# One copy for turned keys and queries, stores by head half, and gathers ahead of the sums in a fused attention and expert kernel

## The chip, the cores and the metric

The kernel runs on one core of a Trainium2 chip, in one launch. The metric is the device time of the execution in microseconds, as a median of several runs. TensorE (PE) multiplies matrices and turns tiles, VectorE (DVE) and ScalarE (ACT) work on tiles lane by lane, GpSimd (POOL) does the same for tiles in SBUF, and SyncE (SP) issues transfers. Each engine takes its instructions in program order and waits for the others by semaphores.

## What is computed

Random feature attention over 8 batches of 8 heads with 576 rows of 64 columns each, whose output goes as 4608 rows of 512 columns into a layer of 8 experts with one expert for each row:

```python
def phi(x):
    proj = np.einsum('bhsd,md->bhsm', x, omega)
    return np.concatenate([np.cos(proj), np.sin(proj)], axis=-1) / np.sqrt(m)
q_p, k_p = (phi(q), phi(k))
kv = np.einsum('bhsm,bhsd->bhmd', k_p, v)
z = np.sum(k_p, axis=2)
num = np.einsum('bhsm,bhmd->bhsd', q_p, kv)
den = np.einsum('bhsm,bhm->bhs', q_p, z)      # |den| kept from zero
x = (num / den)                               # to rows of 512
# experts, on rows x of 512:
logits = xn @ en.T / tau                      # xn, en: rows over their norms
expert_idx = np.argmax(logits, axis=1)
gate_w = probs[np.arange(N), expert_idx]      # softmax of the logits
out[mask] = gate_w[mask, None] * (np.maximum(x[mask] @ w1[e], 0.0) @ w2[e])
```

## The kernel before, in words

**The attention loop.** 32 steps, one for two heads of one batch (head i on partitions 0 to 63, head i + 4 on 64 to 127), run as a pipeline in a loop over n from 0 to 32 (line 1050). The instructions of each engine stand in the order in which the code is written. In iteration n a step's keys and values are multiplied (kv_products(n)), the step before it gets its numerators (num(n - 1), norm(n - 1)), and the step behind it has its keys projected and waved (proj_k(n + 1), frac, wave). "Step n" below is iteration n; VectorE's copy of kvT (line 301) is close to its start.

The raw keys and queries of a step lie in one tile kq; TensorE turns them into PSUM (turns, line 177), from where the projections need them in SBUF. VectorE copies the first 512 columns (copy_k, tile kT, line 189) and ScalarE the other 640 (copy_q, tile qT, line 195). They are read by proj_q and proj_k of the next iteration (lines 208, 225, 234). After the turn ScalarE also makes the sine of the keys (wave, snk) ahead of its copy and their cosine (cok) behind it; VectorE makes the whole turns' remainder (frac, line 251), its absolute value (fold, line 257), and the norm (lines 373 to 375).

The sums of the features over the sequence (z) are made by GpSimd: zsum (lines 277 to 281) adds the nine blocks of snk, then those of cok, in ten instructions; z_turn(n) of the next iteration takes them to TensorE. GpSimd also copies the finished rows to fp16 (to_rows, line 390), sums the logits (sums, lines 422, 424), and issues one of 32 weight pieces in each iteration (weights_in, lines 92 and 98). The order at the end of an iteration is to_rows(n - 1), sums(n - 1), weights_in(n), zsum(n + 1), gathers.

**Routing beside it.** When half of the batches are through, the rows of these are given to experts, in pieces of a few VectorE instructions each, that lie in iterations 9 to 31 (lay_first, line 986; the dictionary pieces). The first piece of an iteration runs ahead of z_turn and kv_out (piece_now), the others behind them (all_pieces). The first 11 of 43 blocks of 128 rows are known then.

**Hand-over.** The rows of the attention go through DRAM: store_rows (line 426) sends a pair of steps from tile xb to x_rows by SP, in odd iterations, two transfers (one for each half of the heads) in a row. gather(j) (line 830) fetches the 128 rows of block j into one of three buffers xin_all by an indirect DMA that GpSimd issues. The same buffers hold v of odd steps until step 29. turn_x(j) (line 867) turns a block on TensorE and copies it to xT by VectorE. In iteration 32 the first block's matmuls begin (hidden(0)).

**Experts.** 43 blocks: hidden(j), 32 matmuls (line 913), result(j), 8 matmuls (line 934), with gathers three blocks ahead, and results scattered to the output by GpSimd (line 947).

The gathers of the first five blocks stand here:

```python
            if NS - 2 <= n < NS:
                turn_x(n + 2 - NS, "dve")
...
            weights_in(n)
            if nx:
                zsum(n + 1, 0)
                zsum(n + 1, 1)
            if n == NS - 3:
                gather(0)
            elif n == NS - 2:
                gather(1)
                gather(2)
```

Of the kernel before, what the change touches and what calls it, by code (L numbers as in the profile page):

```python
# [11 lines left out]
FP32 = mybir.dt.float32  # L12
# [3 lines left out]
I16 = mybir.dt.int16  # L16
AF = mybir.ActivationFunctionType
# [11 lines left out]
def kernel(  # L29
# [12 lines left out]
    nc = tc.nc  # L42
# [6 lines left out]
    P = 128  # L49
# [82 lines left out]
    with tc.tile_pool(name="psA", bufs=1, space=PSUM) as psA, tc.tile_pool(  # L132
# [53 lines left out]

        def copy_k(m):
            t = pa.tile([P, 4 * P], FP32, tag="kT", name="kT", bufs=1)
            nc.vector.tensor_copy(t, qreg[:, 0 : 4 * P])  # L189
            st.setdefault(m + 2, {})["kT"] = t  # L190

        def copy_q(m):
            t = pa.tile([P, 5 * P], FP32, tag="qT", name="qT", bufs=1)
            if m + 1 >= 0:
                nc.scalar.activation(t, qreg[:, 4 * P :], AF.Copy)
                st[m + 1]["qT"] = t
            else:
                nc.scalar.activation(t[0:64, 4 * P :], qreg[0:64, 8 * P :], AF.Copy)
            st[m + 2]["k8"] = t
# [226 lines left out]
        def store_rows(b, a):  # L426
            t = xrow.pop((b, a)).rearrange("p c i d -> p c (i d)").bitcast(I16)
            for hh in range(2):
                f0 = 256 * hh + 128 * a
                ins = nc.sync.dma_start(  # L430
                    out=x_rows[S * b : S * b + S, f0 : f0 + 128].rearrange(
                        "(p c) f -> p c f", c=NCH
                    ),
                    in_=t[64 * hh : 64 * hh + 64],
                )
                late_store(ins, b)
# [545 lines left out]
        def lay(n, every, per):  # L982
            for at, piece in enumerate(every):
                pieces.setdefault(n + at // per, []).append(piece)

        def lay_first():
            r1["rk"] = ar1.take((S1 + 1) * E).rearrange("p (e s) -> p e s", e=E)
            g = [{}, {}]
            for q, n in ((0, 2 * NPAIR + 1), (1, first)):
# [8 lines left out]
                else:  # L998
                    one, two, three = choose_pieces(q)
# [17 lines left out]
                    lay(  # L1017
                        n + 1,
                        [lambda: square_rows(1, (0,)), lambda: square_rows(1, (1,))]
                        + root_pieces(g[q], q, q + 1, ar1)  # L1020
                        + gates_pieces(g[q], q, q + 1, ar1),
                        1,
                    )
# [10 lines left out]

        def piece_now(n):
            todo = pieces.get(n)
            if todo:
                todo.pop(0)()

        def all_pieces(n):  # L1040
            while pieces.get(n):
                piece_now(n)

        def weights_in(n):
            if n < 4 * E:
                emit_weight_piece(n)

        zsum(0, 0)
        zsum(0, 1)
        for n in range(NS + 1):  # L1050
# [3 lines left out]
            if n > 1 and n % 2 == 1:  # L1054
                bb, ii = steps[n - 2]
                store_rows(bb, ii // 2)
# [41 lines left out]
            if nx:  # L1098
                turns(n)
                copy_k(n)  # L1100
                copy_q(n)
                wave(n + 1, "co", "k")
                if n + 2 < NS:
                    load_kq(n + 1)
            if NS - 2 <= n < NS:
                turn_x(n + 2 - NS, "dve")
# [9 lines left out]
            if n > 0:  # L1116
                to_rows(n - 1)
                sums(n - 1)
                if n == NS:
                    store_rows(B - 1, 1)  # L1120
            if n == NS - 2:
                load_v(n + 1)
            weights_in(n)
# [3 lines left out]
            if n == NS - 3:  # L1127
                gather(0)
            elif n == NS - 2:
                gather(1)  # L1130
                gather(2)
            elif n == NS - 1:
                gather(3)
                gather(4)
# [115 lines left out]
```

## Time and profile before

| what | value |
|---|---|
| runs | median 525.76 us of 3 (524.94 to 532.42) |
| the profiled execution | 522.62 us, span 520.9 us |
| TensorE busy | 461.5 us (89%) |
| VectorE busy | 358.4 us (69%) |
| ScalarE busy | 323.0 us (62%) |
| GpSimd busy | 381.6 us (73%) |
| granted clock, mean | 0.98 of full speed |
| moved by DMA | 65.64 MB, mean 126 GB/s |

The shares are means over stages with different limits: the attention loop up to about 311 us, two steps of hand-over, and the experts from 342 us on. So the busy time is read by stage, and single steps by the timeline. A start is counted from the beginning of the span. An idle time in brackets stands ahead of the instruction with what ended it. The granted clock is TensorE's, as a share of 2.4 GHz.

### The profile page before, as it was taken

Reading aid. Unit: us, or ns where it says so; the run is one execution under the profiler, and the core shown is the slowest. Engines: PE = TensorE matmul, PEld = TensorE weight load, DVE = VectorE, ACT = ScalarE, POOL = GpSimd, SP = SyncE. Lnnn points to the kernel's source line nnn. Section 1 sums busy time; section 2 is a strip of 40 time slices with the busy share of each in tenths; the row PEclk is TensorE's granted clock in tenths of the full one; section 3 lists DMA queues with packets and bytes.
Section 4 is the critical chain, followed back from the end, with each engine's and each line's share of the span. In section 5 each row is a group of like instructions: output and inputs, shape, how many; then the busy total and the mean of one; then the engine's idle time right before and its main releaser. Section 6 shows DMA issues by size and latency. Waiting matters only on the chain.

```text
span 520.9 us, 19352 instructions
## 1 busy us (share of the span) xinstructions
PE 461.5 (89%) x8140; PEld 381.3 (73%) x8140; DVE 358.4 (69%) x688; ACT 323.0 (62%) x377; POOL 381.6 (73%) x529
## 2 busy tenths in 40 slices
PE   5898988999889898898989895578999999999993
PEld 4787877878778777777778784476777777777771
DVE  3689877899989899999999995448942323232320
ACT  6778878878877867776878775336643333333331
POOL 2989988999988998889899986836765555555532
PEclk9899999999999999999999998889999999999997
DMA  3568778868767787777676783352333223323110
GB/s 115 136 149 177 152 146 180 162 144 183 164 140 170 162 149 152 158 154 154 146 172 137 155 149 80 76 93 79 90 117 109 96 86 100 101 81 117 62 49 1
DMA packets 57893, 65.64 MB, mean 126 GB/s; under 512 B 29637, under 2 KB 37829, under 8 KB 57808
## 3 DMA queue, kind: packets, MB, share of 16 engines
q0 software_dynamic: 18304, 30.97, 30.5%
q1 hardware_dynamic: 39200, 33.36, 24.9%
q8 instruction: 66, 1.08, 0.9%
q14 instruction: 19, 0.16, 0.1%
q10 hardware_dynamic: 304, 0.08, 0.1%
HBM read 67.90 MB, written 16.01 MB: 161 GB/s over the span
## 4 chain that ended last, share of the span: by engine, by line
PE 50%; DVE 31%; issue 7%; POOL 6%; ACT 2%; DMA 2%; POOLq 0%; SPq 0%; DVEq 0%; ACTq 0%
PE ps L913 13%; PE ps L934 12%; PE ps L291 6%; PE ps L358 6%; DVE sik L251 4%; DVE siq L251 3%; PE ps L181 3%; DVE xa L375 3%; DVE cok L257 3%; PE ps L208 3%; PE ps L225 2%; DVE sq L402 2%; DVE kT L189 2%; PE ps L871 2%; DVE coq L257 2%
## 5 line engine op out<-in xcount | busy, mean ns | idle before, releaser
L913 PEld LDWEIGHTS <-w_sb 128*128 x1376 | 80.3, 98 | 12.7 <-issue 3.0
L358 PE MATMUL ps<-kv,siq 128*64 128x73 f32 x1152 | 76.4, 228 | 13.2 <-DVE kv L340 12.4
L925 DVE TENSOR_SCALAR cok<-ps 128x512 f16<-128x512 f32 x34 | 23.5, 692 | 91.4 <-PE ps L913 91.4
L913 PE MATMUL ps<-kq,w_sb 128*128 128x128 f16 x1376 | 84.0, 219 | 2.6 <-issue 2.6
L934 PE MATMUL ps<-w_sb,cok 128*128 x344 | 81.1, 379 | 0.0
L358 PEld LDWEIGHTS ps<-kv,siq 128*64 128x64 f32 x1152 | 64.5, 135 | 17.9 <-ACT coq L267 12.4
L358 PE MATMUL ps<-kv,coq 128*64 128x73 f32 x1152 | 75.4, 226 | 0.1
L358 PEld LDWEIGHTS ps<-kv,coq 128*64 128x64 f32 x1152 | 65.1, 137 | 0.3 <-ACT coq L267 0.3
L267 ACT ACTIVATE snk<-sik 128x1152 f32<-128x1152 f32 x32 | 37.3, 1167 | 42.6 <-DVE sik L251 42.5
L267 ACT ACTIVATE siq<-siq 128x1152 f32<-128x1152 f32 x32 | 37.2, 1164 | 36.1 <-DVE coq L257 35.6
L832 POOL DMA_INDIRECT xin_all<-rf_x,prm x43 | 46.3, 1077 | 15.3 <-PE ps L871 10.6
L390 POOL CAST xb<-xa 128x576 f16<-128x576 f32 x32 | 35.5, 1110 | 29.7 <-DVE xa L375 28.6
L934 PEld LDWEIGHTS <-cok 128*128 128x128 f16 x344 | 31.9, 98 | 30.7
L251 DVE SCALAR_TENSOR_TENSOR siq<-siq,ps 128x1152 f32<-128x1152 f32 x32 | 43.1, 1346 | 7.2 <-ACT siq L247 6.8
L251 DVE SCALAR_TENSOR_TENSOR sik<-sik,ps 128x1152 f32<-128x1152 f32 x32 | 43.1, 1347 | 3.6 <-ACT sik L247 3.3
L181 PE MATMUL ps<-ident,kq 128*128 128x128 f32 x288 | 39.7, 285 | 6.0 <-DVE siq L251 5.9
L947 POOL DMA_INDIRECT out_dram<-snk,prm x22 | 24.3, 1103 | 27.3 <-ACT snk L946 26.8
L947 POOL DMA_INDIRECT out_dram<-siq,prm x21 | 22.0, 1047 | 30.2 <-ACT siq L946 29.9
L291 PE MATMUL ps<-cok,v 64*64 64x128 f32 x612 | 41.7, 289 | 1.6 <-issue 1.6
L291 PE MATMUL ps<-snk,v 64*64 64x128 f32 x612 | 41.5, 289 | 0.5 <-issue 0.3
L291 PE MATMUL ps<-cok,xin_all 64*64 64x128 f32 x540 | 34.8, 273 | 7.1 <-issue 7.1
L946 ACT ACTIVATE snk<-ps,gpos 128x512 f32<-128x512 f32 x22 | 15.1, 688 | 41.4 <-PE ps L934 41.4
(220 smaller groups left out, 1264.9 us busy)
## 6 DMA issues: line engine op xcount, KB each, us to landing
w_sb<-in_moe_w_dram POOLq DMA_DIRECT2D x32, 512.0 KB, 7.3
kq<-in_k_dram SPq DMA_DIRECT2D x64, 144.0 KB, 3.0
kq<-in_q_dram SPq DMA_DIRECT2D x64, 144.0 KB, 3.2
v<-in_v_dram SPq DMA_DIRECT2D x34, 144.0 KB, 3.0
rf_x<-xb SPq DMA_DIRECT2D x32, 144.0 KB, 7.5
xin_all<-in_v_dram SPq DMA_DIRECT2D x30, 144.0 KB, 3.4
xin_all<-rf_x,prm POOLq DMA_INDIRECT x43, 3.2
out_dram<-snk,prm POOLq DMA_INDIRECT x22, 2.8
```

The source lines that it names most:

```text
L181: nc.tensor.transpose(qreg[:, at : at + P], t[:, j * P : j * P + P], ident)
L251: nc.vector.scalar_tensor_tensor(out=si, in0=si, scalar=CMAGIC, in1=REG[nm], op0=ALU.subtract, op1=ALU.subtract)
L257: nc.vector.tensor_scalar(co.bitcast(I32), st[n]["si" + nm].bitcast(I32), 0x7FFFFFFF, None, ALU.bitwise_and)
L267: nc.scalar.activation(r, t, AF.Sin, bias=pio2 if which == "co" else 0.0, scale=-TWO_PI * SINSC)
L291: nc.tensor.matmul(kreg[64 * half : 64 * half + 64, 512 * hh : 512 * hh + P], lhsT=d["v"][r0 : r0 + 64, c], rhs=ph[r0 : r0 + 64, s * P : s ...
L358: nc.tensor.matmul(nm2[r0 : r0 + 64, a, (c - c0) * W : (c - c0) * W + W], lhsT=ph[:, s * P + r0 : s * P + r0 + 64], rhs=d["kv"][:, half, h ...
L390: nc.gpsimd.tensor_copy(xrow[b, i // 2][:, :, i % 2], st[n]["xa"][:, 0:NCH, 0:64])
L832: ins = nc.gpsimd.indirect_dma_start(out=t, out_offset=None, in_=x_rows[:], in_offset=bass.IndirectOffsetOnAxis(ap=prm[:, j : j + 1], axis=0),
L913: nc.tensor.matmul(h_ps[:, f * P : f * P + P], lhsT=weights(k), rhs=d["xT"][:, c * P : c * P + P], start=(c == 0), stop=(c == 3),)
L925: nc.vector.tensor_scalar(hT[:, 512:], h_ps[:, 512:], 0.0, None, ALU.max)
L934: nc.tensor.matmul(y_ps, lhsT=d["hT"][:, c * P : c * P + P], rhs=weights(NW1 + c), start=(c == 0), stop=(c == NW2 - 1),)
L947: ins = nc.gpsimd.indirect_dma_start(out=out[:], out_offset=bass.IndirectOffsetOnAxis(ap=prm[:, j : j + 1], axis=0), in_=y, in_offset=None ...
```

## The change

Four things are moved or merged.

- **One tile for turned keys and queries.** kT and qT become one tile kqT. In iterations that have routing pieces (9 to 30), ScalarE copies all 1152 columns in one instruction (copy_kq) and VectorE copies none; in the others both copy their part as before.
- **Stores by half.** A pair of steps is stored in two iterations, one half of the heads in each.
- **Order in the first routing.** The squares, roots and gates of the second group are laid ahead of its other pieces, so they come first in iterations 18 to 28. (pieces is no longer emptied, since copy_kq asks whether an iteration has any.)
- **Weights, gathers, turns.** Weight pieces run two iterations earlier, two of them ahead of the loop. gather(0) to gather(2) stand in iterations 29 to 31 ahead of the sums, gather(3) in 31, gather(4) in 32. Blocks 0 and 1 are turned in iterations 31 and 32 instead of 30 and 31.

```diff
+        turned = {}
+
+        def kq_tile(m):
+            if m not in turned:
+                turned[m] = pa.tile([P, 9 * P], FP32, tag="kqT", name="kqT", bufs=1)
+                st.setdefault(m + 2, {})["kT"] = turned[m][:, 0 : 4 * P]
+                st[m + 2]["k8"] = turned[m][:, 4 * P :]
+                if m + 1 >= 0:
+                    st[m + 1]["qT"] = turned[m][:, 4 * P :]
+            return turned[m]
+
         def copy_k(m):
-            t = pa.tile([P, 4 * P], FP32, tag="kT", name="kT", bufs=1)
-            nc.vector.tensor_copy(t, qreg[:, 0 : 4 * P])
-            st.setdefault(m + 2, {})["kT"] = t
+            nc.vector.tensor_copy(kq_tile(m)[:, 0 : 4 * P], qreg[:, 0 : 4 * P])
...
+        def copy_kq(m):
+            nc.scalar.activation(kq_tile(m), qreg, AF.Copy)
...
-        def store_rows(b, a):
-            t = xrow.pop((b, a)).rearrange("p c i d -> p c (i d)").bitcast(I16)
-            for hh in range(2):
+        def store_rows(b, a, hhs):
+            t = xrow[b, a].rearrange("p c i d -> p c (i d)").bitcast(I16)
+            for hh in hhs:
...
                 else:
+                    lay(
+                        n + 1,
+                        [lambda: square_rows(1, (0,)), lambda: square_rows(1, (1,))]
+                        + root_pieces(g[q], q, q + 1, ar1)
+                        + gates_pieces(g[q], q, q + 1, ar1),
+                        1,
+                    )
                     one, two, three = choose_pieces(q)
...
+        weights_in(0)
+        weights_in(1)
         for n in range(NS + 1):
...
-            if n > 1 and n % 2 == 1:
-                bb, ii = steps[n - 2]
-                store_rows(bb, ii // 2)
+            if n > 2:
+                bb, ii = steps[n - 2 - (n + 1) % 2]
+                store_rows(bb, ii // 2, ((n + 1) % 2,))
...
-                copy_k(n)
-                copy_q(n)
+                if pieces.get(n):
+                    copy_kq(n)
+                else:
+                    copy_k(n)
+                    copy_q(n)
...
-            if NS - 2 <= n < NS:
-                turn_x(n + 2 - NS, "dve")
+            if n >= NS - 1:
+                turn_x(n + 1 - NS, "dve")
...
-            weights_in(n)
+            weights_in(n + 2)
+            if NS - 3 <= n < NS:
+                gather(n + 3 - NS)
+            if n == NS - 1:
+                gather(3)
+            elif n == NS:
+                gather(4)
             if nx:
                 zsum(n + 1, 0)
                 zsum(n + 1, 1)
-            if n == NS - 3:
-                gather(0)
-            elif n == NS - 2:
-                gather(1)
-                gather(2)
-            elif n == NS - 1:
-                gather(3)
-                gather(4)
```

How the built programs stand, at three places (lines are those of each program's own file).

GpSimd at the end of iteration 29, before: the weight piece, the ten sums of zsum(30) (zt and zs are its tiles), and the gather of block 0 into xin_all.

```order
L92 DMA w_sb<-in_moe_w_dram 128x2x1024
L277 TENSOR_TENSOR zt<-snk 128x256
L278 TENSOR_TENSOR zt<-zt,snk 128x256
L279 TENSOR_TENSOR zt<-zt,snk 128x256
L280 TENSOR_TENSOR zs_5040<-zt 128x128
L281 TENSOR_TENSOR zs_5040<-zs_5040,snk 128x128
L277 TENSOR_TENSOR zt<-cok 128x256
L278 TENSOR_TENSOR zt<-zt,cok 128x256
L279 TENSOR_TENSOR zt<-zt,cok 128x256
L280 TENSOR_TENSOR zs_5047<-zt 128x128
L281 TENSOR_TENSOR zs_5047<-zs_5047,cok 128x128
L832 DMA xin_all<-rf_x,prm 128x514
```

The same place of the changed kernel, up to the first half of the sums:

```order
L98 DMA w_sb<-in_moe_w_dram 128x4x512
L842 DMA xin_all<-rf_x,prm 128x514
L287 TENSOR_TENSOR zt<-snk 128x256
L288 TENSOR_TENSOR zt<-zt,snk 128x256
L289 TENSOR_TENSOR zt<-zt,snk 128x256
L290 TENSOR_TENSOR zs_4991<-zt 128x128
```

The gather has gone from behind the ten sums to ahead of them, and stands right behind the last weight piece.

VectorE in iteration 20, from the fold of the keys to the fold of the queries, before:

```order
L257 TENSOR_SCALAR cok<-sik 128x1152
L189 COPY kT<-ps 128x512
L373 RECIPROCAL ps<-ps 128x2x5
L374 TENSOR_SCALAR rd<-ps 128x10
L375 TENSOR_TENSOR xa<-ps,rd 128x730
L257 TENSOR_SCALAR coq<-siq 128x1152
```

and in the changed kernel:

```order
L267 TENSOR_SCALAR cok<-sik 128x1152
L383 RECIPROCAL ps<-ps 128x2x5
L384 TENSOR_SCALAR rd<-ps 128x10
L385 TENSOR_TENSOR xa<-ps,rd 128x730
L267 TENSOR_SCALAR coq<-siq 128x1152
```

The copy of kT is gone between the fold and the norm; ScalarE's copy of 640 columns at its place between snk and cok has become one of 1152.

SP from the loads of iteration 29 on, before (kq and v are loads, rf_x the stores of rows and of gates):

```order
L149 DMA kq<-in_k_dram 64x576 x2
L149 DMA kq<-in_q_dram 64x576 x2
L149 DMA v<-in_v_dram 64x576 x2
L430 DMA rf_x<-xb 576x1x128 x4
L821 DMA rf_x<-gate 576x1x2 x4
```

and in the changed kernel:

```order
L149 DMA kq<-in_k_dram 64x576 x2
L149 DMA kq<-in_q_dram 64x576 x2
L440 DMA rf_x<-xb 576x1x128
L149 DMA v<-in_v_dram 64x576 x2
L440 DMA rf_x<-xb 576x1x128 x4
L831 DMA rf_x<-gate 576x1x2 x4
```

Half a store of iteration 30 now stands ahead of the load of v for step 31; it waits for gather(0), since it writes the tensor that the gather reads.

## Rows read from the trace of the kernel before

**Rows 1.** Busy time by stage, us of the stretch first (the header names the columns).
```profile
core 0: us, PE busy (x) PEld busy (x) DVE busy (x) ACT busy (x) POOL busy (x), PEclk, DMA share, GB/s
...
98.80:311.60 212.80, 191.29 (x4077) 166.02 (x4075) 202.95 (x365) 165.23 (x170) 186.51 (x274) 1.00 0.77 157
311.60:342.20 30.60, 18.80 (x365) 16.66 (x361) 16.15 (x33) 12.69 (x13) 21.07 (x32) 0.83 0.39 79
342.20:520.90 178.70, 165.69 (x2010) 124.27 (x2010) 65.77 (x172) 68.30 (x116) 94.41 (x88) 0.98 0.28 84
```

**Rows 2.** The same view for steps 11, 27 and 18 of the attention loop.
```profile
118.43:128.04 9.61, 9.61 (x199) 8.12 (x201) 9.07 (x17) 7.83 (x8) 8.66 (x14) 1.00 0.93 180
...
281.69:291.42 9.73, 9.71 (x203) 8.31 (x199) 9.34 (x18) 7.83 (x8) 8.79 (x14) 1.00 0.81 154
188.12:198.81 10.69, 9.20 (x197) 7.92 (x195) 10.40 (x20) 7.83 (x8) 8.94 (x14) 1.00 0.71 149
```

**Rows 3.** Groups, 98.8 to 311.6 us: busy us, mean ns, idle before and releaser.
```profile
L189 DVE COPY kT<-ps 128x512 f32<-128x512 f32 x21 | 14.3, 679 | 0.0
...
L247 ACT ACTIVATE siq<-ps 128x1152 f32<-128x1152 f32 x21 | 23.3, 1110 | 0.0
...
L267 ACT ACTIVATE snk<-sik 128x1152 f32<-128x1152 f32 x21 | 24.5, 1167 | 31.2 <-DVE sik L251 31.2
...
L267 ACT ACTIVATE siq<-siq 128x1152 f32<-128x1152 f32 x21 | 24.4, 1164 | 14.4 <-DVE coq L257 14.4
...
L390 POOL CAST xb<-xa 128x576 f16<-128x576 f32 x22 | 24.7, 1125 | 13.0 <-DVE xa L375 11.9 <-issue 1.1
...
L279 POOL TENSOR_TENSOR zt<-zt,cok 128x256 f32<-128x256 f32 x21 | 21.4, 1020 | 1.6
...
L279 POOL TENSOR_TENSOR zt<-zt,snk 128x256 f32<-128x256 f32 x21 | 15.8, 753 | 1.6
```

**Rows 4.** Timeline of step 17, VectorE then ScalarE: start us, us, engine, line.
```profile
185.56 0.68 DVE L189 COPY kT<-ps 128x512 f32<-128x512 f32 x1
186.16 0.22 DVE L373 RECIPROCAL ps<-ps 128x10 f32<-128x10 f32 x1
...
184.89 1.17 ACT L267 ACTIVATE snk<-sik 128x1152 f32<-128x1152 f32 x1 [1.63 <-DVE sik L251]
185.96 0.69 ACT L195 ACTIVATE qT<-ps 128x640 f32<-128x640 f32 x1
186.54 1.25 ACT L267 ACTIVATE cok<-cok,pio 128x1152 f32<-128x1152 f32 x1
188.24 1.16 ACT L267 ACTIVATE siq<-siq 128x1152 f32<-128x1152 f32 x1 [0.45 <-DVE coq L257]
```

**Rows 5.** Timeline of GpSimd, steps 29 and 30: last instruction ahead of zsum(30), gather(0).
```profile
312.31 0.74 POOL L92 DMA_DIRECT2D w_sb<-in_moe_w_dram  x1
...
320.81 1.12 POOL L832 DMA_INDIRECT xin_all<-rf_x,prm  x1 [0.54 <-issue]
```

**Rows 6.** Timeline of TensorE, steps 30 and 31 (idle before in brackets).
```profile
323.73 0.61 PE L871 MATMUL ps<-ident,xin_all 128*128 128x128 f16 x4 [5.49 <-DMA xin_all<-rf_x,prm]
...
333.07 0.34 PE L358 MATMUL ps<-kv,coq 128*64 128x73 f32 x4
...
338.29 0.61 PE L871 MATMUL ps<-ident,xin_all 128*128 128x128 f16 x4 [4.88 <-DMA xin_all<-rf_x,prm]
```

**Rows 7.** Timeline of VectorE, step 31: its first instruction, block 1's copy.
```profile
328.10 0.42 DVE L301 COPY kvT<-ps 128x256 f32<-128x256 f32 x1 [1.34 <-PE ps L291]
...
338.93 0.42 DVE L865 COPY kq<-ps 128x512 f16<-128x512 f16 x1 [0.52 <-PE ps L871]
```

**Rows 8.** Busy time by stretch, behind the wait of step 31.
```profile
338.30:342.20 3.90, 3.84 (x76) 3.40 (x76) 2.43 (x6) 0.85 (x1) 1.49 (x3) 0.63 0.36 83
```

**Rows 9.** Landings: the gather at 343.2 us; then loads on SP, 98 to 310 us.
```profile
DMA to landing us min/median/max: 8.7/8.7/8.7
...
DMA to landing us min/median/max: 2.5/3.1/5.6
```

More of the change, by code (lines that the diff above doesn't have):

```diff
@@ L185, in turns @@
                 )
+        turned = {}
[7 more added lines that the diff above has]
+            return turned[m]
         def copy_k(m):
-            t = pa.tile([P, 4 * P], FP32, tag="kT", name="kT", bufs=1)
-            nc.vector.tensor_copy(t, qreg[:, 0 : 4 * P])
-            st.setdefault(m + 2, {})["kT"] = t
+            nc.vector.tensor_copy(kq_tile(m)[:, 0 : 4 * P], qreg[:, 0 : 4 * P])
         def copy_q(m):
-            t = pa.tile([P, 5 * P], FP32, tag="qT", name="qT", bufs=1)
+            t = kq_tile(m)
             if m + 1 >= 0:
-                nc.scalar.activation(t, qreg[:, 4 * P :], AF.Copy)
-                st[m + 1]["qT"] = t
-            else:
-                nc.scalar.activation(t[0:64, 4 * P :], qreg[0:64, 8 * P :], AF.Copy)
-            st[m + 2]["k8"] = t
+                nc.scalar.activation(t[:, 4 * P :], qreg[:, 4 * P :], AF.Copy)
+            else:
+                nc.scalar.activation(t[0:64, 8 * P :], qreg[0:64, 8 * P :], AF.Copy)
+        def copy_kq(m):
+            nc.scalar.activation(kq_tile(m), qreg, AF.Copy)
         KS = [c // 2 + 4 * (c % 2) if c < 8 else 8 for c in range(NCH)]
@@ L1016, in lay_first @@
                     lay(n + 10, rows_of_pieces(r1, 0, K1, ar1), 2)
[L1017 to L1023, printed above, removed]
             one, two, three = choose_pieces(GRP1)
@@ L1033 @@
         lay_first()
+        done = {}
         def piece_now(n):
-            todo = pieces.get(n)
-            if todo:
-                todo.pop(0)()
+            todo = pieces.get(n, [])
+            if done.get(n, 0) < len(todo):
+                todo[done.get(n, 0)]()
+                done[n] = done.get(n, 0) + 1
         def all_pieces(n):
-            while pieces.get(n):
+            while done.get(n, 0) < len(pieces.get(n, [])):
                 piece_now(n)
@@ L1119 @@
                 if n == NS:
-                    store_rows(B - 1, 1)
+                    store_rows(B - 1, 1, (0, 1))
             if n == NS - 2:
                 load_v(n + 1)
-            weights_in(n)
+            weights_in(n + 2)
[5 more added lines that the diff above has]
+                gather(4)
             if nx:
```

## The prediction

> **What bounds the kernel now.** I read three views in this order. First the busy times by stage [rows 1]: from 98.8 to 311.6 us lie 21 attention steps that also carry routing pieces (21 copies of kT there [rows 3]), 10.13 us each. VectorE (DVE) is busy 202.95 us in them, 9.66 of each 10.13; GpSimd (POOL) 8.88, ScalarE (ACT) 7.87, TensorE 9.11. From 342.2 us on the expert blocks run with TensorE busy 165.69 of 178.70 us at a granted clock of 0.98. That stage is bound by its matmuls, and nothing in the change touches them: what the stages ahead of it win, the end wins. Between the two lie 30.6 us, steps 30 and 31, with TensorE busy 18.80 us of them: something waits there.
>
> Second, single steps [rows 2]. Step 18 has 10.40 us of VectorE work and takes 10.69 us; steps 11 and 27 have 9.07 and 9.34 and take 9.61 and 9.73. So a heavy routing step lasts as long as VectorE's work plus some 0.3 us, and near 9.6 us another floor is reached. Third, the instruction groups of these 21 steps [rows 3]: ScalarE waits for VectorE 31.2 + 14.4 us, 2.17 us a step, so it has room; GpSimd waits for VectorE's xa only 11.9 us in all, 0.57 us a step, so without that wait it would still need 9.57 us a step. It is the next floor.
>
> Then the hand-over. gather(0) is issued at 320.81 us, behind the ten sums of zsum(30), which begin when the weight piece of 312.31 has been issued [rows 5]. TensorE, which has reached the turn of block 0 in step 30, stands 5.49 us until it lands, and in step 31 it stands 4.88 us for gather(1) [rows 6]. All the work behind stands with it: on TensorE the products of keys and values, on VectorE the norms and folds.
>
> **The change, part by part.** The wide copy. In each of 22 steps (9 to 30) VectorE loses the copy of kT: from 185.56 to the next instruction at 186.16 it takes 0.60 us [rows 4]. ScalarE's copy grows from 640 to 1152 columns. The wide form does not exist in this trace; the nearest row is ScalarE's own read of the same 1152 PSUM columns, 1.11 us [rows 3], against 0.69 for the narrow copy [rows 4], so +0.42 us. What hides it: in step 17 the cosine of the keys then starts at 186.96 instead of 186.54 and ends at 188.21, while the next sine waits for VectorE's fold until 188.24 today [rows 4]. That fold comes 0.60 sooner; ScalarE's sine is then held by ScalarE itself, but no later than now. Without that cover it would cost 0.42 us a step.
>
> VectorE's work falls from 9.66 to 9.06 us a step. Bounds for the step: the whole 0.60 won (9.53 us, a little under GpSimd's 9.57), or nothing (10.13, if GpSimd keeps its wait). The steps of today with 9.07 to 9.34 us of VectorE work take 9.61 to 9.73, and single steps will stay heavier than the mean, so I take **9.72**: 0.41 us in each of 21 steps, **8.6 us** (bounds 0 and 12.6).
>
> The new order of the pieces in steps 18 to 28 puts a square, root or gate piece ahead of kv and the others behind it. The same instructions run in the same step on the engine that has no idle time there, so I put it at nothing; a heavier first piece delays kv by up to the difference, at most some 0.5 us in a few steps, up to 2 us either way. Half stores: the same 32 transfers, one in each step instead of two in every other, on SP, with buffers that are reused four steps later. I put this at nothing too; a gain in evenness or a delay stays within 1 us.
>
> Gathers ahead of the sums. gather(0) now stands in step 29 behind the last weight piece, so at about 313.4 on the old time scale. A gather issued at 343.2, the first behind a weight piece, landed 8.7 us after its issue [rows 9]; so by 322.1. The turn of block 0 has moved to step 31, gather(1) to step 30 ahead of zsum(31), and the turn of block 1 to step 32. Both waits go. Step 30, which takes 16.5 us (311.6 to 328.10 [rows 1, 7]), becomes an ordinary step: −6.8 us against 9.72. Step 31 loses the wait of 4.88 us; and the stretch behind it, 3.90 us at a granted clock of 0.63 [rows 8], because TensorE had stood idle ahead of it, runs at the upper of the two levels, 2.4 GHz. At full clock it would be 2.5 us; I count 1.2 of the 1.4. Step 31: −6.1 us.
>
> What these moves cost. The turn of block 1 now stands in step 32 between the numerators and the next block's matmuls: 0.61 us on TensorE and 0.42 for VectorE's copy, with hand-offs **+1.1 us** [rows 6, 7]. SP's half store in step 30 waits for gather(0), and behind it on SP stands the load of v for step 31. It goes out near 322.7 and lands after 3.1 us, 5.6 at most [rows 9], with two issues between 326.4 and 329. Step 31 starts near 321.3; its numerators end 5.3 us after the start (328.10 to 333.07 plus 0.34 [rows 6, 7]), block 0's turn adds 0.6, so v is wanted at 327.2: 0 to 1.8 us, I take **+0.4**. On GpSimd each gather pushes the sums behind it by 1.4 us. zsum(30) would end at 321.7 and is wanted near 322.5; zsum(31) ends some 10.4 us into step 31 and is wanted about 11.4 us after that step's start. Both fit with a margin of about 1 us, which is what comes late next. Two weight pieces ahead of the loop take 1.5 us from GpSimd at the start, where its sums have that much slack; I count **+0.3**. Later the earlier pieces only free steps 30 and 31.
>
> Sum: −8.6 − 6.8 − 6.1 + 1.1 + 0.4 + 0.3 = **−19.7 us**. The profiled execution took 522.62 us (520.9 of it span), so 502.9 by that. It is 3.1 us below the median 525.76 of the runs shown, by which the sum is 506.1. A repeat can lie at either; I take **504.5**.
>
> **Rivals.** (1) GpSimd takes VectorE's place and routing steps win nothing. For it: its 9.57 us a step, and its sums over cok, 1.02 us where their twins over snk take 0.75 [rows 3], so it is slowed by something that runs beside it. Against it: steps 11 and 27 pass in 9.6 to 9.7 us. Then only the hand-over is won, 11.1 us: 511.5 to 514.7, say **513**. The Trainium skill (SBUF — State Buffer, section SBUF: two separate sides) has the mechanism: VectorE and GpSimd share a port pair as an exclusive lock, held for a whole instruction by a 2-port VectorE operation. By that rule the removed copy, which reads PSUM, never held the pair, and the folds that do hold it stay, so GpSimd gains no time from this change. The slow sums agree with it; how often the lock falls badly at another spacing no row here shows.
>
> (2) The sums come late at the hand-over. If gather(0) at the head of GpSimd's queue has to wait (for the gate stores of step 29, or for the keys' products that read the buffer it overwrites), zsum(30) and (31), to_rows and the next gathers all shift. With a margin of about 1 us, a wait of 4 us costs some 3 in step 31 and more in 32: 15 us won instead of 19.7, **509**.
>
> (3) Slower: the wide copy is late. It stands between the sine and the cosine of the keys, and TensorE's next query projection waits for it, with GpSimd's sums and the folds behind. If reading 1152 columns took 2.5 us or more, ScalarE's chain of a step would grow by 1.4 beyond today's cover; at 21 steps that passes the 11.1 us of the hand-over when a step reaches 10.66 us. At 3 us it would give about **535**. Against it: the same read takes 1.11 us in two instructions of every step.
>
> (4) Everything won: 12.6 us in the routing steps and no price at the hand-over, 25 us: **499**.
>
> **How the numbers follow.** My forecast 0.67 (499.5 to 510.5), rival (1) 0.15, (2) 0.10, (4) 0.05, (3) 0.03. The range 498 to 514 leaves out (3), part of (1) and the edges. A measurement of this kernel tells about 2% from no change, here 515.2 us. The forecast, (2), (4) and most of (1) lie below it: faster 0.88, within 2% 0.09 (the rest of (1) and a mishap of both halves), slower 0.03.
>
> **What the changed profile would show.** The wide copy at 1.1 us with 22 instances; the step period from 98.8 us on at 9.6 to 9.8 us, VectorE near 9.1 us busy in it, and ScalarE's wait for VectorE's fold ahead of the query's sine nearly gone. If (1) holds, GpSimd's wait for xa stays at 0.5 us and the period above 10. No wait of TensorE for a gather in steps 30 and 31, step 30 under 10.5 us, step 31 near 8.5, the clock at full through both; if (2) holds, TensorE waits for zs there. Wrong for good would be a step period above 10.2 or a new wait of over 3 us in steps 29 to 32.

## The result, and the profile after

The changed kernel takes 506.28 us (median of 503.63, 504.32, 508.25 and 509.27), the kernel before 525.81 us (524.94 to 532.42): a ratio of 0.9604, 95% interval 0.9503 to 0.9705. The prediction was 504.5 us, range 498 to 514, with 0.88 on faster. The profiled execution of the changed kernel took 503.63 us, span 501.9 us (before 522.62 and 520.9). Some executions of a kernel fall into a slower group, some per cent above the others; every median below is of the faster ones.

The busy times by stage, with the columns of [rows 1]: routing steps, step 30, step 31, the rest. A step starts here where VectorE begins its copy of kvT.

```profile
core 0: us, PE busy (x) PEld busy (x) DVE busy (x) ACT busy (x) POOL busy (x), PEclk, DMA share, GB/s
97.96:303.86 205.90, 189.85 (x4073) 164.39 (x4071) 191.12 (x343) 171.95 (x170) 186.68 (x274) 1.00 0.77 161
303.86:312.80 8.94, 8.63 (x195) 7.62 (x193) 8.37 (x17) 7.85 (x9) 8.14 (x12) 1.00 0.62 125
312.80:322.92 10.12, 8.28 (x170) 7.25 (x166) 5.68 (x15) 4.31 (x5) 9.23 (x15) 0.83 0.32 73
322.92:501.90 178.98, 166.06 (x2014) 124.54 (x2014) 66.12 (x175) 68.90 (x116) 96.33 (x92) 0.99 0.26 82
```

On the same marks the kernel before has 77.28 us in steps 1 to 8, 212.71 in the 21 routing steps, 16.53 and 14.11 in steps 30 and 31, and 178.69 behind.

| stretch | before | after | difference | predicted |
|---|---|---|---|---|
| steps 1 to 8 | 77.28 | 76.30 | −1.0 | +0.3 |
| 21 routing steps | 212.71 | 205.90 | −6.8 | −8.6 |
| step 30 | 16.53 | 8.94 | −7.6 | −6.8 |
| step 31 | 14.11 | 10.12 | −4.0 | −6.1 |
| from step 32 on | 178.69 | 178.98 | +0.3 | +1.1 (and +0.4 for the load of v) |

The sum is right, its parts are off by up to 2.1 us. The groups that answer to [rows 3], over the 21 routing steps (busy us, mean ns, idle before and releaser):

```profile
L277 ACT ACTIVATE snk<-sik 128x1152 f32<-128x1152 f32 x21 | 24.5, 1168 | 32.1 <-DVE sik L261 32.1
...
L277 ACT ACTIVATE siq<-siq 128x1152 f32<-128x1152 f32 x21 | 24.2, 1153 | 0.7 <-DVE coq L267 0.7
...
L209 ACT ACTIVATE kqT<-ps 128x1152 f32<-128x1152 f32 x21 | 23.3, 1111 | 0.0
...
L267 DVE TENSOR_SCALAR cok<-sik 128x1152 int32<-128x1152 int32 x21 | 20.2, 961 | 2.1
L400 POOL CAST xb<-xa 128x576 f16<-128x576 f32 x22 | 20.1, 912 | 5.9 <-DVE xa L385 5.9
```

The wide copy takes 1111 ns (predicted 1.1 us). ScalarE's wait for the query's fold went from 14.4 to 0.7 us: the copy lies where that wait was, as foretold. GpSimd's wait for xa fell from 11.9 to 5.9 us. Steps 11, 27 and 18 of the changed kernel, beside [rows 2]:

```profile
117.65:126.48 8.83, 8.83 (x195) 7.82 (x197) 8.00 (x16) 7.75 (x9) 8.18 (x13) 1.00 0.83 184
275.30:284.41 9.11, 9.11 (x195) 7.95 (x197) 8.39 (x16) 6.65 (x7) 7.95 (x13) 1.00 0.63 137
183.95:194.48 10.53, 9.55 (x199) 8.12 (x197) 9.88 (x19) 8.55 (x9) 9.37 (x15) 1.00 0.86 176
```

The light steps 11 and 27 won 0.78 and 0.62 us, to below the floor of 9.6 us that the prediction had read; the heavy step 18 won 0.16 us, although VectorE lost 0.52 us of work in it.

At the hand-over the waits of [rows 6] for gathers are gone. A smaller one has come in step 31. TensorE's timeline (idle before in brackets), then its busy time and granted clock in stretches of 2 us:

```profile
314.58 0.39 PE L337 MATMUL ps<-ones,zs 64*128 64x1 f32 x4 [0.89 <-POOL zs L291]
...
316.20 0.31 PE L368 MATMUL ps<-kv,siq 128*64 128x73 f32 x3 [0.72 <-DVE kv L350]
```
```profile
310.80:312.80 2.00, 1.98 (x56) 1.00 0.06 15
312.80:314.80 2.00, 1.11 (x14) 1.00 0.62 122
314.80:316.80 2.00, 1.28 (x31) 1.00 0.41 99
316.80:318.80 2.00, 2.00 (x45) 0.59 0.27 74
318.80:320.80 2.00, 2.00 (x36) 0.56 0.31 74
```

TensorE waits 0.89 us for the sums, then 0.72 us for kv, and the 4 us behind run at a clock of 0.59 and 0.56, near the lower of its two levels, 1.2 GHz. On GpSimd, the gather that stands ahead of the sums, and the last of these sums:

```profile
305.68 1.12 POOL L842 DMA_INDIRECT xin_all<-rf_x,prm  x1 [0.31 <-issue]
...
314.07 0.46 POOL L291 TENSOR_TENSOR zs<-zs,cok 128x128 f32<-128x128 f32 x1
```

### The profile page after: what moved, and what is told of

The parts are those of the page before. It is cut to its first block, busy times and chain, and to the rows that moved or that the text cites. A ratio compares the mean times of both kernels' runs of the same rounds, so it can differ in the third digit from the quotient of the medians.

```text
span 501.9 us, 19312 instructions
## 1 busy us (share of the span) xinstructions
PE 460.2 (92%) x8140; PEld 379.0 (76%) x8140; DVE 344.4 (69%) x666; ACT 329.3 (66%) x377; POOL 381.5 (76%) x529
## 4 chain that ended last, share of the span: by engine, by line
PE 48%; DVE 28%; POOL 12%; issue 6%; DMA 2%; ACT 2%; POOLq 0%; SPq 0%; DVEq 0%; ACTq 0%
PE ps L923 14%; PE ps L944 13%; PE ps L301 6%; PE ps L368 5%; DVE sik L261 4%; DVE siq L261 4%; DVE xa L385 3%; PE ps L218 3%; DVE cok L267 3%; PE ps L235 3%; POOL zt L287 2%; POOL zt L288 2%; PE ps L181 2%; POOL zt L289 2%; PE ps L881 2%
## 5 line engine op out<-in xcount | busy, mean ns | idle before, releaser
L923 PEld LDWEIGHTS <-w_sb 128*128 x1376 | 80.4, 98 | 12.5 <-issue 2.9
L368 PE MATMUL ps<-kv,siq 128*64 128x73 f32 x1152 | 77.7, 230 | 10.2 <-DVE kv L350 9.4
L368 PE MATMUL ps<-kv,coq 128*64 128x73 f32 x1152 | 76.8, 229 | 0.2
L218 PEld LDWEIGHTS ps<-omT,kqT 64*128 64x128 f32 x576 | 44.0, 192 | 15.5 <-issue 14.5
L218 PE MATMUL ps<-omT,kqT 64*128 64x128 f32 x576 | 48.5, 282 | 0.6 <-DVE emb_n L495 0.6
L957 POOL DMA_INDIRECT out_dram<-snk,prm x22 | 24.2, 1101 | 27.4 <-ACT snk L956 26.9
L301 PE MATMUL ps<-cok,v 64*64 64x128 f32 x612 | 39.1, 276 | 2.5 <-issue 2.4
L956 ACT ACTIVATE siq<-ps,gpos 128x512 f32<-128x512 f32 x21 | 14.4, 687 | 39.6 <-PE ps L944 39.6
```

What stands on the lines that cost most here:

```text
L218: nc.tensor.matmul(kreg[:, s * P : s * P + P], lhsT=t[r0 : r0 + 64, j * P : j * P + P], rhs=omT[r0 : r0 + 64], start=True, stop=True,)
L301: nc.tensor.matmul(kreg[64 * half : 64 * half + 64, 512 * hh : 512 * hh + P], lhsT=d["v"][r0 : r0 + 64, c], rhs=ph[r0 : r0 + 64, s * P : s ...
L368: nc.tensor.matmul(nm2[r0 : r0 + 64, a, (c - c0) * W : (c - c0) * W + W], lhsT=ph[:, s * P + r0 : s * P + r0 + 64], rhs=d["kv"][:, half, h ...
L923: nc.tensor.matmul(h_ps[:, f * P : f * P + P], lhsT=weights(k), rhs=d["xT"][:, c * P : c * P + P], start=(c == 0), stop=(c == 3),)
L956: nc.scalar.activation(y, y_ps, AF.Copy, scale=gpos[:, j : j + 1])
L957: ins = nc.gpsimd.indirect_dma_start(out=out[:], out_offset=bass.IndirectOffsetOnAxis(ap=prm[:, j : j + 1], axis=0), in_=y, in_offset=None ...
```

## The experiments

All twelve runs beside the two kernels. Steps are in us, from the kvT copies of each run's trace. "Stalls" is the time in steps 1 to 8 that TensorE stood over 0.4 us at a stretch in the products of keys and values without a releaser ("issue" in the profile). Each ratio is to the kernel before on the same chip, which took 527.94 us beside e1 to e4, 524.92 beside e5 to e8 and 535.09 beside e9 to e12. On this last chip everything from step 32 on took 8 us longer, so these four are compared among themselves.

| run | median | ratio to before, interval | 1 to 8 | routing | 30 | 31 | stalls |
|---|---|---|---|---|---|---|---|
| before | 525.81 | | 77.3 | 212.7 | 16.5 | 14.1 | 4.3 |
| changed | 506.28 | 0.9604 (0.9503 to 0.9705) | 76.3 | 205.9 | 8.9 | 10.1 | 1.8 |
| e1 narrow copies | 514.53 | 0.9754 (0.9698 to 0.9810) | 76.0 | 216.9 | 9.6 | 9.4 | 2.5 |
| e2 wide only | 522.50 | 0.9842 (0.9749 to 0.9935) | 79.9 | 210.4 | 15.9 | 15.4 | 4.1 |
| e3 hand-over only | 516.03 | 0.9772 (0.9696 to 0.9848) | 80.7 | 214.9 | 9.5 | 8.6 | 5.1 |
| e4 both | 513.12 | 0.9691 (0.9621 to 0.9761) | 83.1 | 209.8 | 10.8 | 10.7 | 4.7 |
| e5 turns back | 504.47 | 0.9628 (0.9549 to 0.9708) | 76.9 | 206.9 | 10.3 | 8.0 | 2.4 |
| e6 gathers behind sums | 508.63 | 0.9707 (0.9631 to 0.9783) | 77.3 | 207.8 | 9.0 | 12.4 | 1.1 |
| e7 cast on ScalarE | 501.85 | 0.9565 (0.9510 to 0.9619) | 78.5 | 202.3 | 9.8 | 7.5 | 0.0 |
| e8 last piece early | 507.85 | 0.9677 (0.9625 to 0.9728) | 75.9 | 204.9 | 8.9 | 13.4 | 2.1 |
| e9 double stores | 516.9 | 0.9663 (0.9586 to 0.9740) | 76.5 | 209.0 | 10.5 | 10.4 | 2.6 |
| e10 old piece order | 513.47 | 0.9600 (0.9569 to 0.9630) | 77.2 | 207.9 | 9.0 | 10.1 | 1.5 |
| e11 cast from step 9 | 505.94, 506.10 | two executions, no interval | 77.7 | 201.1 | 9.3 | 7.9 | 2.6 |
| e12 changed again | 512.19 | 0.9610 (0.9559 to 0.9660) | 75.9 | 206.6 | 9.0 | 10.2 | 2.0 |

### The wide copy: taken back, and alone

```diff
-                if pieces.get(n):
-                    copy_kq(n)
-                else:
-                    copy_k(n)
-                    copy_q(n)
+                copy_k(n)
+                copy_q(n)
```

> The changed kernel with the turned keys copied by VectorE again in every step (half stores, piece order and hand-over stay as changed). Theory (VectorE sets the pace of the routing steps, and the wide copy is what relieves it): the 21 routing steps go back from 205.9 us to 211 to 214, step 30 from 8.9 to about 9.5, steps 31 and 32 stay; whole kernel 506.3 + 7 = 513 (511 to 515). Rival (the gain of the routing steps came from the order of the pieces or from the half stores): the routing steps stay within 1.5 us of 205.9 and the kernel at 506. Second rival (GpSimd alone is the pace there): VectorE's busy time rises by about 14 us but the steps stay at 9.8.

Measured: 514.53 us. The routing steps take 216.9 us, 11.0 more than in the changed kernel and more than expected. 4.0 of it lies in steps 20 and 21 (24.2 us for 20.2): one stall of 1.95 us, and the clock behind it, which the windows of step 21 show:

```profile
218.50:222.50 4.00, 4.00 (x26) 0.50 0.66 110
222.50:226.50 4.00, 4.00 (x74) 0.67 0.69 137
226.50:231.30 4.80, 4.80 (x107) 1.00 0.30 81
```

The other 19 steps take 7.0 us more, 0.37 each: the theory's size. The second rival is out too: VectorE has 12.7 us more work in the 21 steps, and the steps do not stay as they were.

The other way round, the kernel before with the wide copy alone:

> The kernel before with nothing but the wide copy by ScalarE in iterations 9 to 30. Theory: the 21 routing steps fall from 212.7 to 206 (205 to 208), steps 30 and 31 keep their waits for the gathers (16.5 and 14.1, step 30 perhaps half a microsecond less); whole kernel 525.8 - 7 = 519 (517 to 521). Rival (piece order or half stores carry the gain): the routing steps stay above 211 and the kernel at 525.

Measured: 522.50 us, 5.4 below the kernel before beside it (527.94), where 7 was expected. The routing steps are only 2.3 us shorter, because step 18 takes 15.2 us. Its waits (total, times, longest):

```profile
PEld ps L181 <- issue: 3.6, 1, 3.6
PE ps L181 <- DMA kq<-in_q_dram: 3.4, 1, 3.4
ACT kqT L209 <- PE ps L181: 3.0, 1, 3.0
```

TensorE waits for queries that SP loads too late: in SP's order two row stores and two gate stores stand ahead of the load. The other 20 steps fall from 202.0 to 195.3 us, 0.34 each. So both directions give 0.34 to 0.37 us a step for the copy, and the wide copy alone exposes a transfer that had its time before.

### The hand-over alone, and both without the rest

The hand-over part put into the kernel before:

```diff
-            weights_in(n)
+            weights_in(n + 2)
+            if NS - 3 <= n < NS:
+                gather(n + 3 - NS)
...
-            if NS - 2 <= n < NS:
-                turn_x(n + 2 - NS, "dve")
+            if n >= NS - 1:
+                turn_x(n + 1 - NS, "dve")
```

> The kernel before with nothing but the hand-over part (weight pieces two iterations earlier, gathers ahead of the sums, turns of blocks 0 and 1 one iteration later). Theory: routing steps unchanged at 212 to 213, step 30 falls from 16.5 to 9 to 9.8, step 31 from 14.1 to about 10.1 (sums late by 0.9 us as in the changed kernel), from step 32 on within 1 us; whole kernel 525.8 - 11.6 = 514 (512 to 516). Rival (VectorE slower in the hand-over without the wide copy, so that steps 30 and 31 take over 10.5 each): 516 or more. Second rival (the weights moved earlier slow the first steps by transfers): steps 1 to 8 longer than 77.3 by over 1 us.

Measured: 516.03 us, 11.9 us below the kernel before beside it (527.94). Steps 30 and 31 take 9.5 and 8.6 us for 16.5 and 14.1: the hand-over part wins 12.5 us by itself. Step 31 is 1.5 us shorter than in the changed kernel, although TensorE waits for the sums there too, 1.21 us: the clock stays up (step 31, columns as above).

```profile
326.71:335.29 8.58, 6.43 (x168) 5.73 (x164) 5.66 (x15) 3.90 (x4) 7.85 (x13) 1.00 0.29 73
```

The first rival is out. The second got what it asked for, steps 1 to 8 at 80.7 us, though their cause is a stall and the clock behind it. TensorE's timeline in step 3 and its windows in step 4:

```profile
50.58 0.43 PE L291 MATMUL ps<-cok,xin_all 64*64 64x128 f32 x2 [2.12 <-issue]
```
```profile
52.00:54.00 2.00, 2.00 (x20) 0.50 0.90 141
54.00:56.00 2.00, 2.00 (x22) 0.50 1.00 215
56.00:58.00 2.00, 2.00 (x32) 0.50 0.01 1
58.00:60.00 2.00, 2.00 (x51) 0.92 0.00 0
```

Both edits together, without the half stores and the piece order:

> The changed kernel without the half stores and without the new order of the pieces: the wide copy and the hand-over part alone. Theory (these two edits are worth nothing): routing steps 205 to 207, steps 30 and 31 as in the changed kernel (8.9 and 10.1), whole kernel 506 to 507.5; if the half stores are worth anything it shows in steps 1 to 8, whose sum was 77.3 before and 76.3 after. Rival (they carry 2 us or more): 508.5 or more, in steps 18 to 28 if it is the order of the pieces, in the steps of the double stores if it is the stores.

Measured: 513.12 us, 6.8 over the changed kernel's median. Some 2 us of that is the chip, on which the kernel before took 527.94 for 525.81, and the intervals of the two ratios overlap. So the time makes it doubtful that the other two edits are worth nothing, and does not settle it. Steps 1 to 8 have 4.7 us of stalls and a step 6 of 12.0 us at a clock of 0.72; step 18 waits 2.2 us for queries again.

### Which of the two small edits it is

The changed kernel with both halves stored in one iteration:

```diff
-            if n > 2:
-                bb, ii = steps[n - 2 - (n + 1) % 2]
-                store_rows(bb, ii // 2, ((n + 1) % 2,))
+            if n > 1 and n % 2 == 1:
+                bb, ii = steps[n - 2]
+                store_rows(bb, ii // 2, (0, 1))
```

> The changed kernel with both halves of a pair of rows stored in one iteration again (wide copy, piece order and hand-over as changed). In the runs so far the kernels with double stores (before, wide copy only, hand-over only, both together) had 4.1 to 5.1 us of TensorE stalls in the products of keys and values in steps 1 to 8, those with half stores 1.1 to 2.5; and the two with double stores and wide copy waited 2.2 and 3.4 us for a load of queries in step 18. Theory S (two stores at once hold up the transfers behind them): stalls of 4 us or more in steps 1 to 8, a wait of 2 us or more for queries in step 18, and a lower granted clock in the step behind a stall of about 2 us; whole kernel 4 to 8 us over the changed one, 510 to 514. Rival C (the order of the pieces does it): the kernel within 1.5 us of the changed one, no wait in step 18.

> The changed kernel with the routing pieces of the second group in the order of before (half stores, wide copy and hand-over as changed). Theory S (the stores carry it, the piece order nothing): within 1.5 us of the changed kernel, 505 to 508, stalls in steps 1 to 8 below 2.5 us, no wait for queries in step 18. Rival C: 509 or more, with the wait for queries in step 18 as in the kernel of wide copy and hand-over alone.

(The second only moves the block that lays the square, root and gate pieces back to its old place.) For scale, the changed kernel ran beside them:

> The changed kernel once more, beside the three others. Expected: 506.3 within 1.5 us; routing steps 205 to 208, steps 30 and 31 together 18.5 to 19.5, TensorE stalls below 2.5 us in steps 1 to 8.

Measured: changed again 512.19 us (511.72 to 516.85), old piece order 513.47 (512.73 to 513.61), double stores 516.9 (513.91 to 520.9). The piece order is worth nothing that shows. The double stores cost 4.7 us by the medians, with overlapping intervals; the expected waits came at other places. Stalls in steps 1 to 8 were 2.6 us, not 4, and step 18 did not wait; but step 9 stalled 2.76 us and took 13.0 us, and in step 30 two transfers were late (waits of that step):

```profile
PEld ps L181 <- issue: 2.3, 1, 2.3
POOL xin_all L842 <- DMA rf_x<-gate: 2.1, 1, 2.1
PE ps L181 <- DMA kq<-in_q_dram: 2.1, 1, 2.1
```

On SP that is one queue. In the changed kernel the last loads ahead of step 30 were issued at 302.24 and 302.88 us, 1.6 and 1.0 us before the step began; with double stores at 308.81 and 309.45, 0.5 and 1.1 us after it had. Over all traces, the five kernels with double stores have 2.6 to 5.1 us of stalls in steps 1 to 8 (mean 4.1), the nine with half stores 0 to 2.6 (mean 1.8). That the stores cause them is not shown: e4 and e9 issue the same instructions up to step 8 and have 4.7 and 2.6 us, and e9 differs from e12 (2.0) in the stores alone.

What TensorE waits for in these stalls, the packets of the instruction queue (q8, 65 or 66 of 16 KB in each trace) make likely. In the 14 traces, steps 1 to 31 have 90 stalls of this kind over 0.4 us, and each of them ends 1.2 to 2.0 us after such a packet has landed; of moments taken at random 13% lie so. In step 5 of the kernel before, the packet lands at 68.36 us and the stall of 2.19 us ends at 69.79. So TensorE most likely waits for its own instructions there; what makes them late, no run settles.

### The hand-over taken apart

Turns of blocks 0 and 1 back in steps 30 and 31, gathers ahead of the sums:

> The changed kernel with the turns of blocks 0 and 1 back in iterations 30 and 31 (gathers stay ahead of the sums). In the changed kernel the gather of block 0 was issued at 305.68 and landed at 311.88, behind the last weight piece on the same queue, and TensorE ended step 30's numerators at about 309.9. Theory: TensorE waits for it in step 30 by about 2 us, in step 31 nothing (that gather took 2.9 us), the turn in step 32 costs less by 0.6; whole kernel 507 to 508.5. Rival (the later place of the turns is what the hand-over won): step 30 above 13 us, kernel 511 or more. Second rival (the place of the gathers is enough, that of the turns is free): no wait, 506.

Measured: 504.47 us, no worse than the changed kernel. In step 30 TensorE waits 1.4 us for the gather (theory: 2), the step takes 10.3; then the sums have caught up, step 31 takes 8.0 at full clock, and the two together 18.3 us for 19.1. The later turns are worth nothing in this kernel: with the gathers earlier, 1.4 us is all that is left of the waits of 5.49 and 4.88 us. From step 32 on it takes 178.07 us, 0.9 less than the changed kernel.

Gathers back behind the sums, turns late. In this kernel the gather of block 4 stands ahead of the turn of block 1, with which it shares a buffer, so block 1 works on the wrong rows; the amount of work is the same:

> The changed kernel with the gathers back behind the sums over the sequence, in the iterations that they had before (turns stay one iteration later, weight pieces two earlier). Theory (the wait for the gathers is gone by the later turns alone, and the gathers ahead only push the sums back): block 0's gather issues near 313, lands near 316, 4 us ahead of its turn; the sums of step 31 come 1.4 us earlier, so that TensorE's wait of 0.9 us for them goes and step 31 falls from 10.1 to about 9.3; whole kernel 505 to 506. Rival (the gathers must stand ahead): a wait for a gather of 2 us or more in step 31 or 32, kernel 508 or more.

Measured: 508.63 us, with no wait for a gather in steps 30 and 31, and none for the sums. So the later turns remove the waits for the gathers too, without the earlier gathers. But step 31 takes 12.4 us. Its waits, and SP's timeline:

```profile
PEld ps L301 <- DMA v<-in_v_dram: 3.2, 2, 2.5
PE ps L301 <- DMA v<-in_v_dram: 2.8, 2, 2.3
```
```profile
319.32 0.55 SPq L440 DMA_DIRECT2D rf_x<-xb  x1
319.97 2.11 SPq L149 DMA_DIRECT2D v<-in_v_dram  x2
```

The gather of block 0 landed at 319.31 us; SP's half store, which waits for it, went at 319.32, and the load of v behind that. This is the term that the prediction had at +0.4 us. In the changed kernel the gather landed at 311.88, the store went at 311.89 and nothing waited. The place of the gathers does matter, for the load queued behind a store that waits for them.

The last weight piece a step earlier. The expectation names the kernel with the cast on ScalarE as its base; the kernel that ran stands on the changed kernel, with the cast on GpSimd:

```diff
-            weights_in(n + 2)
+            if n != NS - 3:
+                weights_in(n + 2)
+            if n == NS - 4:
+                weights_in(n + 3)
```

> The kernel of the run with the cast on ScalarE, and the last weight piece issued one iteration earlier still, so that none stands ahead of the gather of block 0. Theory: that gather lands about 3 us after its issue in place of 6.2, GpSimd starts the sums of step 31 about 1.1 us earlier, the half store behind the gather and the load of v behind that come 4 us earlier; nothing of it is on the path once the cast has left GpSimd, so the time is that of the run before it within 1 us. Rival (the sums are still late there): step 31 falls by another 0.5 to 1 us.

Measured: 507.85 us, step 31 at 13.4. The gather landed in 3.0 us as expected, yet GpSimd waited 2.7 us for the gate store before it could issue it, and the sums behind came late by 3.0 us (waits of steps 30 and 31):

```profile
PE ps L337 <- POOL zs L291: 3.0, 1, 3.0
POOL xin_all L842 <- DMA rf_x<-gate: 2.7, 1, 2.7
```

That is the mechanism of rival 2: a wait of 2.7 us on GpSimd's queue went with 3.3 us more in step 31, part of it at a clock of 0.50.

### GpSimd's part

The cast to 16 bits on ScalarE, in every step and from step 9 on. The first half store of a pair moves behind the cast with it (not shown in the cut):

```diff
             if n > 1:
+                to_rows(n - 2, True)
                 squares(n - 2)
...
-                to_rows(n - 1)
                 sums(n - 1)
```

> The changed kernel with the cast of the normalised rows (0.66 to 1.12 us of GpSimd in every step) moved to ScalarE, right ahead of its squaring of the same rows, where ScalarE waits for VectorE anyway; the first half store of a pair goes behind it. Theory (GpSimd paces the steps that have few routing pieces and those without, VectorE the ones with many): steps 1 to 8 fall from 76.3 to about 73, the light routing steps (10, 11, 14 to 16, 27, 28) by 0.3 each, the heavy ones (17 to 25, 29) by no more than 0.2 each, step 31 by 0.7 since the sums come earlier; whole kernel 499 to 501. Rival (GpSimd paces no step, VectorE and TensorE do): within 1.5 us of 506. Second rival (ScalarE's 0.7 us more delays the key sine in the heavy steps, since its wait there is no slack but the chain from VectorE): routing steps 208 or more, kernel 508 or more.

> The changed kernel with the cast of the rows on ScalarE from block step 8 on and on GpSimd before. With the cast on ScalarE everywhere the routing steps took 202.3 us and steps 30 and 31 17.3 (205.9 and 19.1 in the changed kernel), but steps 1 to 8 78.5 (76.3), because there ScalarE's part of the chain got longer by 0.7 us. Theory: steps 1 to 8 at 76 to 77, routing steps 202 to 203, steps 30 and 31 17 to 18; whole kernel 499 to 501, some 2 us below the kernel with the cast on ScalarE everywhere. Rival (the gain in the routing steps came from the calmer transfers of that run and not from GpSimd): 204.5 or more in the routing steps, 504 or more.

Measured: 501.85 us with the cast on ScalarE in every step. With it from step 9 on 505.94 and 506.10, 6 us under the changed kernel beside it. The routing steps fall to 202.3 and 201.1 us (205.9 and 206.6), steps 30 and 31 together to 17.3 and 17.2 (19.1 and 19.2): step 31 at 7.5 and 7.9 with the clock at 1.00, since the sums come in time. Steps 1 to 8 do not fall, against the theory; they take 78.5 without a single stall. VectorE waits 11.9 us in them for ScalarE's first pass over the projected queries (line 257), 8.3 in the changed kernel, so ScalarE may have taken GpSimd's place there, and whether GpSimd paced them stays open. Where the routing steps won is not where the theory had it either: e11 beside e12 won 4.8 us in the ten heavy steps (17 to 25 and 29), with 4.5 us less work on VectorE, and 0.7 in the eleven lighter ones, though GpSimd's work fell by 6.2 us there. The stage and two groups of it, in the changed kernel beside it (e12):

```profile
97.59:304.19 206.60, 189.79 (x4075) 164.59 (x4075) 189.59 (x344) 172.07 (x170) 187.34 (x274) 1.00 0.78 160
```
```profile
L267 DVE TENSOR_SCALAR cok<-sik 128x1152 int32<-128x1152 int32 x21 | 19.4, 926 | 2.1
...
L434 POOL TENSOR_TENSOR la<-la,xa 128x72 f32<-128x72 f32 x16 | 5.2, 326 | 0.0
```

and with the cast on ScalarE from step 9 on:

```profile
99.42:300.51 201.09, 189.94 (x4073) 164.50 (x4071) 183.94 (x344) 184.99 (x190) 173.76 (x254) 1.00 0.79 164
```
```profile
L267 DVE TENSOR_SCALAR cok<-sik 128x1152 int32<-128x1152 int32 x21 | 17.7, 843 | 2.1
...
L438 POOL TENSOR_TENSOR la<-la,xa 128x72 f32<-128x72 f32 x16 | 12.0, 750 | 10.6 <-DVE xa L385 10.6
```

VectorE has the same instructions and 183.94 us of work, where the changed kernel beside it had 189.59: its fold of the keys takes 843 ns for 926 there (961 in the first profile), 1.7 us of the fall. And GpSimd's add of the logits, which now comes first behind xa, beside VectorE's next fold, takes 750 ns where it took 326 behind the cast. The trace shows how: 15 of the 16 adds start 0.16 us after the start of that fold, and end 0.19 us after its end, 776 to 780 ns long; the one that does not fall beside a fold takes 327 ns. The two engines lengthen each other's instructions. The Trainium skill (SBUF — State Buffer, section SBUF: two separate sides) has VectorE and GpSimd share one port pair as an exclusive lock; the 326 and 750 ns of the same add agree with it.

## Why the prediction was right, point by point

**What bounds.** VectorE in the heavy routing steps: e1 and e2 give the copy back as 0.34 to 0.37 us a step, and in e11 these steps fell with VectorE's work. GpSimd as the next floor at 9.57 us was wrong. Its work over the 21 steps stayed as it was (186.51 us before, 186.68 after), yet light steps fell to 8.83 and 9.11 us, and with 6.2 us less for GpSimd (e11) the lighter steps won only 0.7. What paces the lighter ones was not settled. TensorE is busy all of steps 11 and 27, but it was so before as well [rows 2]; these windows are cut by VectorE's copy and need not hold the same matmuls (step 11 has eight of 512 columns before, six after).

**Routing steps, −8.6 us; −6.8 came.** The term that was off is the mean: all 21 were priced by an average VectorE load of 9.06 us, 4.5 us for the eleven lighter ones and 4.1 for the ten heavy ones (17 to 25 and 29). VectorE's work did fall nearly so far, to 9.10 a step (11.7 us in all), but 8.3 us of that lies in the lighter steps, which won 4.1 us: there its work is not all that counts, and stalls of 1.45 and 1.44 us stand in steps 9 and 26. In the heavy ones the work fell by 3.4 us, not 6.0, and they won 2.7; so most of the miss lies there. The copy is not what fell short: against e1, which differs in it alone, VectorE's work in the heavy steps falls by the whole 6.0 us (103.05 to 97.08), and in e2 by 6.8 (100.47 to 93.72). What gave 2.6 us back lies in the other edits or in the spread between executions (95.77 in e12, the same kernel), and was not settled. The cover for the wide copy nearly held: ScalarE's wait for the fold is used up to 0.7 us; what now waits for ScalarE is TensorE's weight loads for the wide copy, 3.0 us in 13 waits, and VectorE for the query's fractions, 3.8 us for 1.6 before.

**Half stores, 0 ± 1 us; probably the wrong step.** They were weighed by the number of transfers. What they change is how long SP's queue is ahead of a load. e2 and e4 wait 3.4 and 2.2 us for queries in step 18, e9 2.1 us in step 30, the kernels with half stores nowhere over 1 us. That is part of the price of the shorter steps: what was loaded in time for a step of 10.7 us was late for one 0.4 shorter. Their worth is 4.7 us by the medians of e9 and e12, not settled by the intervals. The routing steps won 1.8 us less than said and step 31 2.1 less; steps 1 to 8 and step 30 won 1.3 and 0.8 more, and what the half stores are worth was left out. So the sum came out right partly by luck.

**Piece order, 0 ± 2 us.** Right: e10 and e12 differ by 1.3 us.

**Step 30, −6.8; −7.6 came.** Right, an ordinary step.

**Step 31, −6.1; −4.0 came.** The prediction gave the sums a margin of about 1 us. They were 0.89 us late, and the 4 us behind ran at a clock of 0.56 to 0.59, where full clock was foretold. That is rival 2 in a small form. Without late sums the step takes 7.5 to 8.0 us (e5, e7, e11), about the 8.0 that the term meant; with sums late by 1.21 us but full clock 8.6 (e3); with sums late by 0.5 us and a clock of 0.82 over the step 9.4 (e1); with sums late by 0.9 and a clock of 0.83 10.1 to 10.2 (changed, e10, e12). So more of the 2.1 us lost is the clock than the wait.

**Behind.** The turn of block 1 in step 32 cost 0.3 us against the kernel before and 0.9 against e5, where it stands in step 31; 1.1 was foretold. The load of v cost nothing, as its gather landed 8.0 us after the start of step 30 (311.88) and not 10.5 (322.1 on the old scale): 6.2 us after its issue, not 8.7.

**Rivals.** (1) failed as told, since the mean period is 9.80 us; but GpSimd does slow VectorE: with the cast taken off it, VectorE's work over the routing steps is 5.7 to 6.7 us less (e11, e7). (3) is out: 1111 ns.

## What to carry over

A mean load prices a loop only if its steps are alike: cost the heavy and the light ones apart, and check the fall of the work in each. When steps get shorter, look at each queue for the transfer that was just in time, and at what stands ahead of it. A wait of TensorE of 0.9 us ahead of dense work went with a loss of twice that through the clock (step 31), and an instruction moved off GpSimd can pay on VectorE (e7, e11).

## What was not expected of the hardware

Behind a stall of about 2 us TensorE ran at half clock (0.50) for 6 us in e3 and for over 4 us in e1, and a step took 12.0 and 12.8 us; the kernel before had a stall of 2.19 us in step 5 and kept its clock, so not each one does it. In step 31 waits for the sums of 0.52 us (e1) and 0.89 us (changed) were followed by a lower clock, and one of 1.21 us (e3) was not. What decides it stays open. These stalls and what follows them may be a part of why single executions of one kernel lie 5 us apart; that was not taken apart.
